# Block 1 of the first segment's input: one load issued by GpSimd instead of two on the sync queue

## The chip, the cores and the metric

The kernel runs on one core of one Trainium2 chip. The metric is the time of one execution on the device, in microseconds (us). A core has TensorE (PE in the profile; PEld is its weight loads), VectorE (DVE), ScalarE (ACT), GpSimd (POOL) and SyncE (SP), which issues transfers. ScalarE and GpSimd can issue transfers as well.

## The reference

Attention with a compressive memory, a gated unit beside it, and a product of the two added to the input. Cut to what matters:

```
xn = layernorm(x)                               # x: 2048 x 640, bf16
q, k, v = xn @ wq, xn @ wk, xn @ wv             # 32 heads of 20
for s in range(4):                              # segments of 512 rows
    p     = softmax(q_s k_s^T * 20**-0.5 + causal mask)
    a_mem = phi(q_s) M / (phi(q_s) z + 1e-6)    # phi(t) = t + 1 if t > 0 else exp(t)
    o_s   = sigmoid(beta) * a_mem + (1 - sigmoid(beta)) * (p v_s)
    M, z  = M + phi(k_s)^T v_s, z + sum(phi(k_s))
s = o @ wo
g = silu((sigmoid(xn @ w_gate) * (xn @ w_up)) @ w_down)   # inner width 1536
out = x + s * g
```

The layer norm at the head is what this change touches: every matmul of a segment needs its normalised and transposed input.

## The kernel before, in words

The rows are worked in four segments of 512, each of four blocks of 128 rows (one row per partition). The order of instructions is written out by hand: each engine executes what is assigned to it in the order in which the code names it, and a wait holds everything behind it on that engine. For the segments after the first a planner with due times mixes attention with the dense matmuls; the first segment has a written-out opening, and that is where the change lies.

`load_x(n, a, b, cols, eng)` (L128 to L132) loads blocks a to b of segment n into the tile `xt`, on the sync queue unless another engine is named; half a block's columns are 80 KB, a whole block 160 KB. `load_wv(half, eng)` (L149 to L151) loads one half of the columns of Wv, 400 KB. `load_w` (L135) loads a whole weight.

The opening issues (L154 to L164), in the order of the code: block 0 in two halves (sync, ScalarE), block 1 in two halves (both sync), the first half of Wv between them (ScalarE), block 2 (sync), block 3 (ScalarE), the second half of Wv, Wk, Wq and beta (sync). GpSimd issues no transfer; it makes constants: `epsc` (L167, the bias of ScalarE's square roots), `mhalf`, `ident` (L173 and L174, the identity for TensorE's transposes), the columns of ones beside V (L184, L185) and `o6` (L506). Then it waits for block 3's normalisation (L191).

TensorE begins with 68 small matmuls on zeros (L640), which do no work of the result. For each block, `half_stats0(j, i)` (L651) takes the statistics of one half's columns on VectorE, `moments0` (L654) joins them, `root0` (L657, ScalarE) and a reciprocal (L662, VectorE) give the inverse deviation, `norm0` (L665) normalises, `transpose0` (L675, TensorE; copies at L678 and L680 on VectorE and ScalarE) transposes, and `do_V` (psv, L121; copy at L352) and then `proj` (psq, L121) multiply. The written order on VectorE runs block 1's first statistics ahead of block 0's normalisation:

```
half_stats0(0, 0); half_stats0(0, 1); moments0(0); root0(0)
half_stats0(1, 0)
norm0(0, (0, CUT), (CUT, D))
half_stats0(1, 1)
moments0(1)
```

The Wg and Wu loads are issued by ScalarE later, between its square roots and copies (L135).

Of the kernel before, what the change touches and what calls it, by code (L numbers as in the profile page):

```python
# [10 lines left out]
D = 640  # L11
# [11 lines left out]
HD = D // 2  # L23
# [52 lines left out]
def kernel(  # L76
# [14 lines left out]
    nc = tc.nc  # L91
# [36 lines left out]
    def load_x(n, a=0, b=4, cols=slice(0, D), eng=nc.sync):  # L128
        if n not in xt_of:
            xt_of[n] = lnp.tile([P, 4, D], BF, name="xt4", bufs=3)  # L130
        src = x2[n * L:(n + 1) * L, :].rearrange("(j p) d -> p j d", p=P)
        eng.dma_start(xt_of[n][:, a:b, cols], src[:, a:b, cols])  # L132
# [16 lines left out]
    def load_wv(half, eng):  # L149
        hs = slice(half * HD, (half + 1) * HD)  # L150
        eng.dma_start(Wv[:, :, hs], A_wv[:, hs].rearrange("(c p) n -> p c n", p=P))  # L151
# [1 line left out]

    load_x(0, 0, 1, slice(0, HD))  # L154
    load_x(0, 0, 1, slice(HD, D), nc.scalar)
    load_x(0, 1, 2, slice(0, HD))
    load_wv(0, nc.scalar)
    load_x(0, 1, 2, slice(HD, D))
    load_x(0, 2, 3)
    load_x(0, 3, 4, eng=nc.scalar)  # L160
    load_wv(1, nc.sync)
# [844 lines left out]
```

## Time and profile before

| what | value |
|---|---|
| median of 3 runs | 317.6 us (317.12 to 317.6) |
| profiled execution | 317.32 us, span 315.6 us |
| TensorE busy | 310.0 us, 98% of the span |
| VectorE, ScalarE busy | 226.0 and 226.8 us, 72% each |
| GpSimd busy | 131.9 us, 42% |
| granted TensorE clock | 1.0 |

Times within the profile count from the start of the span. In the order in time a row gives start, length, engine, line, operation, what it writes and reads, and in brackets the idle time before it with what ended it. The engines' names with a q (SPq, ACTq) are their issues of transfers; the length of such a row is that of the issue, not of the transfer. In the DMA view q1 is the sync queue and q10 ScalarE's, with packets, megabytes and the time that they took as a share of 16 engines.

### The profile page before, as it was taken

The page shows a single profiled execution, that of the slowest core. Times are in us where ns is not written, and L with a number is a line of the kernel's source. Part 1 is how long each engine was busy: PE and PEld are TensorE (multiplying, and loading weights), DVE is VectorE, ACT ScalarE, POOL GpSimd, SP SyncE. Part 2 cuts the span into 40 slices and gives each one's busy share as a digit, 9 for nine tenths or more (in the row PEclk, how much of TensorE's full clock was granted, in tenths as well). Part 3 has the DMA queues.
Part 4 walks back from the last instruction along what each step waited for, and adds up shares of the span by engine and source line. Part 5 has one row for each costly group of instructions (what it writes and reads, how often), then busy time and mean ns, then how long its engine had stood idle before and what let it go on. Part 6 is the DMA issues. An engine that isn't in the chain of part 4 may idle for free.

```text
span 315.6 us, 10262 instructions
## 1 busy us (share of the span) xinstructions
PE 310.0 (98%) x4329; PEld 167.6 (53%) x4329; DVE 226.0 (72%) x512; ACT 226.8 (72%) x231; POOL 131.9 (42%) x227
## 2 busy tenths in 40 slices
PE   7999999999999999999999999999999999999995
PEld 4644445665545445654665454545466655444673
DVE  5573455765868988878879989788777776644575
ACT  3724478778798776778897869679897775777730
POOL 2580035535262534435453364444534353525313
PEclk9999999999999999999999999999999999999999
DMA  7984886410741363504954355139524000280202
GB/s 228 367 351 151 298 214 171 128 42 2 218 154 58 98 150 111 124 23 151 261 168 116 119 98 162 51 111 213 172 84 125 19 23 30 79 159 11 86 21 85
DMA packets 55390, 41.27 MB, mean 131 GB/s; under 512 B 25968, under 2 KB 53968, under 8 KB 55344
## 3 DMA queue, kind: packets, MB, share of 16 engines
q1 hardware_dynamic: 52800, 35.87, 41.0%
q10 hardware_dynamic: 2544, 4.75, 4.1%
q8 instruction: 34, 0.56, 0.7%
q14 instruction: 12, 0.10, 0.1%
HBM read 19.98 MB, written 14.73 MB: 110 GB/s over the span
## 4 chain that ended last, share of the span: by engine, by line
PE 96%; DMA 1%; DVE 1%; SPq 0%; issue 0%
PE up L121 12%; PE yp L121 11%; PE gp L121 11%; PE psq L121 10%; PE Sps L548 8%; PE gp L125 6%; PE yp L125 6%; PE up L125 6%; PE ApsT L572 6%; PE psv L121 5%; PE psq L125 4%; PE sp L121 3%; PE sp L125 3%; PE psv L125 2%; PE sp L532 2%; DMA xt<-in_A_x_dram 1%
## 5 line engine op out<-in xcount | busy, mean ns | idle before, releaser
L556 ACT ACTIVATE pt<-Sps 128x2048 bf16<-128x2048 f32 x80 | 150.3, 1878 | 40.8 <-PE Sps L548 39.5
L558 POOL TENSOR_SCALAR_AFFINE_SELECT pt<-pt 128x512 bf16<-128x512 bf16 x128 | 82.5, 660 | 155.9 <-ACT pt L556 155.8
L435 DVE SCALAR_TENSOR_TENSOR hT<-tg,up 128x512 bf16<-128x512 bf16 x48 | 32.6, 679 | 23.9 <-PE up L121 9.7
L121 PE MATMUL up<-xnT,Wu 128*128 128x512 bf16 x159 | 42.5, 380 | 0.0
L121 PE MATMUL gp<-xnT,Wg 128*128 128x512 bf16 x152 | 40.1, 380 | 0.0
L424 ACT ACTIVATE tg<-gp 128x512 bf16<-128x512 f32 x48 | 28.6, 595 | 14.4 <-PE gp L121 10.5
L121 PE MATMUL yp<-Wd,hT 128*128 128x320 bf16 x246 | 38.2, 300 | 0.0
L548 PE MATMUL Sps<-QT,KT 23*128 23x384 bf16 (+3 forms) x512 | 32.0, 301 | 0.0
L121 PEld LDWEIGHTS <-hT 128*128 128x128 bf16 x246 | 22.7, 98 | 11.3 <-issue 3.0
L580 DVE STREAM_TRANSPOSE tb<-ApsT 128x512 f32<-128x512 f32 x31 | 22.0, 711 | 4.2 <-PE ApsT L572 4.1
L452 DVE SCALAR_TENSOR_TENSOR aa<-t,yp 128x320 bf16<-128x320 bf16 x32 | 15.3, 478 | 13.5 <-ACT t L451 13.4
L125 PE MATMUL gp<-xnT,Wg 128*32 128x512 bf16 x352 | 24.4, 380 | 0.0
L572 PE MATMUL ApsT<-pt,V 128*32 128x512 bf16 (+2 forms) x496 | 23.5, 299 | 0.0
L121 PEld LDWEIGHTS <-Wu 128*128 128x128 bf16 x159 | 14.2, 98 | 17.4 <-issue 4.0
L121 PEld LDWEIGHTS <-Wg 128*128 128x128 bf16 x152 | 14.1, 98 | 15.8 <-issue 1.9
L125 PE MATMUL yp<-Wd,hT 128*32 128x320 bf16 x552 | 21.9, 300 | 0.0
L125 PE MATMUL up<-xnT,Wu 128*32 128x512 bf16 x324 | 21.7, 380 | 0.0
L548 PEld LDWEIGHTS <-KT 23*128 23x128 bf16 x512 | 9.2, 92 | 23.4 <-issue 23.4
L592 DVE STREAM_TRANSPOSE obT<-ob 128x256 f32<-128x256 f32 x31 | 13.5, 434 | 11.1 <-POOL ob L589 11.0
L589 POOL TENSOR_TENSOR ob<-tb,rb 128x320 bf16<-128x320 f32 x27 | 19.9, 737 | 2.3
L121 PE MATMUL psq<-xnT,Wq 128*128 128x512 bf16 x85 | 19.5, 379 | 0.0
L572 PEld LDWEIGHTS <-V 128*32 128x32 bf16 x496 | 14.4, 97 | 8.1 <-ACT tg L424 0.2
(124 smaller groups left out, 448.0 us busy)
## 6 DMA issues: line engine op xcount, KB each, us to landing
KT<-Kd SPq DMA_DIRECT2D x32, 80.0 KB
QT<-Qd SPq DMA_DIRECT2D x32, 80.0 KB
out_dram<-xt SPq DMA_DIRECT2D x14, 160.0 KB
Wg<-in_B_w_gate_dram ACTq DMA_DIRECT2D x1, 1920.0 KB
Wu<-in_B_w_up_dram ACTq DMA_DIRECT2D x1, 1920.0 KB
xt<-in_A_x_dram SPq DMA_DIRECT2D x3, 640.0 KB
Wd<-in_B_w_down_dram SPq DMA_DIRECT2D x1, 1920.0 KB
Od<-odot SPq DMA_DIRECT2D x3, 640.0 KB
```

The source lines that it names most:

```text
L121: nc.tensor.matmul(out_, lhsT=lhsT, rhs=rhs, start=start, stop=stop, skip_group_check=True)
L125: nc.tensor.matmul(out_[cols], lhsT=lhsT[:, cols], rhs=rhs, start=start, stop=stop, tile_position=(0, 32 * r), skip_group_check=True)
L424: nc.scalar.activation(tg[:], gp[:], ACT.Tanh, scale=0.5)
L435: nc.vector.scalar_tensor_tensor(out=h[:], in0=seg[n]["tg"][:], scalar=1.0, in1=up[:], op0=ALU.add, op1=ALU.mult)
L452: nc.vector.scalar_tensor_tensor(out=s["aa"][j][:, hs], in0=t2[:], scalar=1.0, in1=yp[:], op0=ALU.add, op1=ALU.mult)
L548: nc.tensor.matmul(Sps[:, r, c0:c0 + ncol], lhsT=KT[32 * r:32 * r + DH + 3, g, kb * P:(kb + 1) * P], rhs=QT[32 * r:32 * r + DH + 3, g, q0: ...
L556: nc.scalar.activation(pt[:, :, 0:ntot], Sps[:, :, 0:ntot], ACT.Exp, scale=SCALE)
L558: nc.gpsimd.affine_select(out=pt[:, :, c0:c0 + P], in_=pt[:, :, c0:c0 + P], compare_op=ALU.is_ge, fill=0.0, base=0, pattern=[[0, 4], [1, P ...
L572: nc.tensor.matmul(ps[32 * r:32 * r + 32, q0:L], lhsT=Vflat[n % 2][:, off:off + 32], rhs=t[:, r, c0:c0 + ncol], start=(i == 0), stop=(i == ...
L580: nc.vector.transpose(tb[:].rearrange("p h e -> p (h e)"), ps[:].rearrange("p (a t b) -> p a b t", t=32, b=2))
L589: eng.tensor_tensor(to, of, by, op=ALU.mult)
L592: nc.vector.transpose(s["obT", g // 4][:, g % 4, :].bitcast(F32), ob[:].rearrange("p a e b -> p (a e b)").bitcast(F32))
```

## The change

Block 1 of segment 0 is loaded as one transfer of 160 KB that GpSimd issues, at the place of the first of the two halves on the sync queue; the second half's issue goes. As the program is built, that issue is GpSimd's first instruction after the start, ahead of `epsc`; the statistics of block 1's first half wait for this transfer, and those of its second half for nothing more. On the sync queue block 2 comes next after block 0's half. Of the compute instructions none is added, removed or moved on any engine.

```diff
--- before.py
+++ after.py
@@ -153,9 +153,8 @@
 
     load_x(0, 0, 1, slice(0, HD))
     load_x(0, 0, 1, slice(HD, D), nc.scalar)
-    load_x(0, 1, 2, slice(0, HD))
+    load_x(0, 1, 2, eng=nc.gpsimd)
     load_wv(0, nc.scalar)
-    load_x(0, 1, 2, slice(HD, D))
     load_x(0, 2, 3)
     load_x(0, 3, 4, eng=nc.scalar)
     load_wv(1, nc.sync)
```

## The prediction

> **What bounds the kernel now.** I read the page first, for the busy shares and the clock.
>
> ```profile
> span 315.6 us, 10262 instructions
> PE 310.0 (98%) x4329; PEld 167.6 (53%) x4329; DVE 226.0 (72%) x512; ACT 226.8 (72%) x231; POOL 131.9 (42%) x227
> PEclk9999999999999999999999999999999999999999
> ```
>
> TensorE is busy for 310.0 of 315.6 us. Only 5.6 us are not matmul, so an edit of the first loads can matter only by moving the time at which the matmuls get going. The second view is the chain of waits that ended last, in its first 30 us (start, length, what):
>
> ```profile
> 1.71 3.93 DMA xt<-in_A_x_dram
> 5.66 0.50 DVE st L651
> ...
> 7.55 0.45 PE pT L675 x5
> 8.01 1.45 PE psv L121 x10
> 9.46 0.36 PE pT L675 x5
> 9.82 1.36 PE psv L121 x10
> 11.18 0.30 PE pT L675 x5
> 11.47 2.13 PE psv L121 x15
> 13.61 10.79 PE psq L121 x50
> ```
>
> From 7.55 us on the chain is TensorE without a gap (each row starts where the one before ends, up to 24.40). Whatever moves the transposes of block 1 moves the end by the same amount. And the chain begins with one of the two transfers that the edit removes: the second half of block 1, issued at 1.71, landed at 5.64. So the edit sits on the chain, and the question is when block 1 lands.
>
> The third view is the order in time of the first microseconds (start, length, engine, line, operation, and the idle time before it with its cause):
>
> ```profile
> 0.79 0.41 ACTq L132 DMA_DIRECT2D xt<-in_A_x_dram  x1
> 0.79 0.10 POOL L167 MEMSET epsc<- 128x2 f32 x1 [0.29 <-POOLq L990]
> 0.79 1.82 SPq L132 DMA_DIRECT2D xt<-in_A_x_dram  x4
> ...
> 1.14 0.29 POOL L174 TENSOR_SCALAR_AFFINE_SELECT ident<-ident 128x128 bf16<-128x128 bf16 x1
> 1.23 0.46 ACTq L151 DMA_DIRECT2D Wv<-in_A_wv_dram  x1
> ...
> 1.72 0.55 ACTq L132 DMA_DIRECT2D xt<-in_A_x_dram  x1
> ...
> 2.65 0.44 SPq L151 DMA_DIRECT2D Wv<-in_A_wv_dram  x1
> 3.15 0.89 DVE L651 BATCH_NORM_STATS2 st<-xt 128x6 f32<-128x320 bf16 x2 [1.96 <-DMA xt<-in_A_x_dram]
> ...
> 3.59 0.20 ACT L169 ACTIVATE epsc<-epsc 128x1 f32<-128x1 f32 x1
> ...
> 4.19 0.44 DVE L651 BATCH_NORM_STATS2 st<-xt 128x6 f32<-128x320 bf16 x1
> ...
> 4.64 0.16 DVE L662 RECIPROCAL rs<-rs 128x1 f32<-128x1 f32 x1
> 4.84 0.64 DVE L665 TENSOR_SCALAR xn<-xt,mv,rs 128x384 bf16<-128x384 bf16 x2
> ...
> 5.30 0.52 PE L675 MATMUL pT<-ident,xn 128*128 128x128 bf16 x5
> ...
> 5.66 0.49 DVE L651 BATCH_NORM_STATS2 st<-xt 128x6 f32<-128x320 bf16 x1 [0.19 <-DMA xt<-in_A_x_dram]
> ...
> 6.26 0.85 PE L121 MATMUL psv<-Wv,xnT 128*128 128x320 bf16 x5 [0.23 <-ACT xnT L680]
> ...
> 7.55 0.45 PE L675 MATMUL pT<-ident,xn 128*128 128x128 bf16 x5 [0.39 <-DVE xn L665]
> ```
>
> VectorE takes its work in the written order: the two statistics of block 0 (3.15), the first half of block 1 (4.19), then the reciprocal and normalisation of block 0 (4.64 to 5.48), then the second half of block 1 (5.66). The whole wait for block 1 is the 0.19 us before 5.66.
>
> The fourth view is the DMA queues, by packets in a stretch of time. q1 is the sync queue and q10 ScalarE's; the first fence is 2.9 to 4.1 us, the second, the sum over all queues, 4.1 to 5.64 us.
>
> ```profile
> q10 hardware_dynamic: 510, 0.32, 90.5%
> q1 hardware_dynamic: 40, 0.02, 6.6%
> ```
>
> ```profile
> DMA packets 567, 0.48 MB, mean 314 GB/s; under 512 B 54, under 2 KB 567, under 8 KB 567
> ```
>
> For 1.2 us q1 moved almost nothing, 40 packets to q10's 510, though block 1's second half had been issued on it at 1.71. The engines worked off the first half of Wv (issued by ScalarE at 1.23) instead. The sizes, from the list of issues in the page:
>
> ```profile
> Wv<-in_A_wv_dram ACTq DMA_DIRECT2D x1, 400.0 KB
> ...
> xt<-in_A_x_dram SPq DMA_DIRECT2D x3, 80.0 KB
> ...
> xt<-in_A_x_dram SPq DMA_DIRECT2D x1, 160.0 KB
> ```
>
> So what stands on one queue when Wv's turn comes waits for nearly all of Wv. Block 1's first half, issued on SP some 0.46 us earlier (four issues in 1.82 us), got ahead of it; the second half did not.
>
> **The change, part by part.**
>
> *SP.* Two issues go, 2 x 0.455 = 0.91 us of the queue. Block 2 moves up from 2.2 to about 1.24, the second half of Wv from 2.65 to about 1.70, and Wk and Wq follow at about 2.15 and 2.6; as built, neither of these two waits for an earlier load any more. This gains nothing: block 2 is used behind block 1, and the weights stand behind block 2 and Wv in a ring that is full anyway. One thing does change: block 2 (160 KB) now takes the turn ahead of Wv that block 1's first half (80 KB) had.
>
> *GpSimd.* One issue is added, ahead of epsc, mhalf, ident, the ones columns and o6. The trace has no issue by GpSimd. The nearest rows are 0.41 to 0.55 us (ScalarE's) from below; from above I allow 2 us. Its cover: epsc is made at 0.79 and used at 3.59, 2.7 us of slack; ident is ready at 1.43 and used at 5.30. So the engine's own time costs nothing up to 2.7 us, and the excess after that would.
>
> *VectorE's wait.* This is the price. The statistics of the first half now wait for the whole block, and the reciprocal and normalisation of block 0 are queued behind that wait, with TensorE's transposes and ScalarE's copies of block 0 behind them. Let T be the landing of the whole block. If T is 4.19 or less, the second half's statistics follow at 5.47 and no wait is left: 5.47 - 5.66 = -0.19 us, and that is the most the edit can give, since VectorE is then back to back. If T is later, they start at T + 1.28 (5.47 - 4.19), and the shift of the chain is T + 1.28 - 5.66 = T - 4.38. TensorE's own waits (0.23 and 0.39 us) move along with it, since they wait for the same VectorE chain. So nothing takes the shift up again, and it arrives at the end whole. For the longer idle time of TensorE before its first real matmuls I put down no loss of clock: the PEclk row shows 9 in the first slice too, with TensorE idle for its first 1.24 us.
>
> *T itself.* The transfer is issued at 0.79, where epsc stood. SP's first issue, at the same moment, has no packet on record in the first 1.8 us and 17 in the first 1.9 us; in the first 2.5 us q1 has 142, and in the first 2.75 us q10 has 148:
>
> ```profile
> DMA packets 0, 0.00 MB, mean 0 GB/s; under 512 B 0, under 2 KB 0, under 8 KB 0
> ...
> q1 hardware_dynamic: 17, 0.01, 3.2%
> ...
> q1 hardware_dynamic: 142, 0.09, 15.4%
> ...
> q10 hardware_dynamic: 148, 0.09, 10.3%
> ```
>
> So SP's queue needs about 1.05 us from issue to the first data. GpSimd's can't well be quicker: data from 1.8 us at the earliest. The point that decides is when Wv's turn comes on the engines. q10 had its half of block 0 (128 rows) and some small packets done by 2.75, so Wv begins at about 2.7 to 2.9. If block 1's descriptors are there by then, it goes with blocks 0 and 2 and T is about 3.7 to 4.2. If not, it stands where the old second half stood, behind Wv, and T is at least that row's 5.64. It is also later by what stands ahead of it in addition: 80 KB (block 2 for a half block) and 80 KB more of its own, 160 KB at the 314 GB/s of the row, 0.51 us. So T lies between 5.64 and 6.15 and the shift between 1.26 and 1.77 us; I take the middle, 1.5. GpSimd may add up to 0.9 to 1.1 us to SP's 1.05 and still be in time. I take it that it is not: the generation of 128 rows' descriptors by a general engine, and their way to the queues, has to fit into twice the time of the hardware path, cold, as the first thing that GpSimd does.
>
> *A rule that speaks otherwise.* The Trainium skill, in "DMA: Bandwidth & Descriptors", section "Anatomy of one DMA — SWDGE (gpsimd) path", gives a transfer from GpSimd as about 2.0 us fixed plus bytes over 436 GB/s. By that page's figures (an estimate) 160 KB issued at 0.79 land at 0.79 + 2.0 + 0.38 = 3.2, and the sum would be -0.19 us; that fit has no full queue beside it, and no row here shows a GpSimd transfer. Another rule speaks against the edit: the Trainium skill's "SBUF — State Buffer", section "Summary: rules for kernel authors", says to issue such a transfer from ACT or SP, because VectorE's two-port operations starve GpSimd's making of descriptors. Here VectorE is idle for the 1.96 us before 3.15, so by the trace that rule has little to act on in the time that decides.
>
> **The sum.** The profiled execution took 317.32 us, its span 315.6, so 1.7 us lie outside. 317.32 + 0 (SP, GpSimd) + 1.5 = 318.8. The profiled execution is 0.28 below the median of the three runs, 317.6; from that it would be 319.1. I give 318.9.
>
> **The rivals.**
>
> 1. Block 1 behind Wv (my forecast): 317.32 + 1.26 = 318.6 to 317.6 + 1.77 = 319.4. For it: the 1.2 us in which q1 was shut out. Against it: the 0.9 us or more of allowance. Chance 0.54.
>
> 2. Block 1 in time, not slower. The descriptors are ready before 2.7 us, or a third queue gets a share beside Wv instead of waiting for its end. In time gives -0.19: 317.1 to 317.4. A share: from about 3.0 at half of 314 GB/s, 160 KB take 1.0 us, and with the 0.6 us by which block 0's first half landed (3.15) after its 128 packets had gone (2.5) T is 4.6, +0.2: 317.5 to 317.8. In time, Wv's first half moves back by 240 KB, 0.8 us, and takes up the 0.8 us between its landing and its use at 6.26 (a row of the order in time, and one of SP's own waits):
>
> ```profile
> 5.46 0.64 SPq L164 DMA_DIRECT2D beta_b<-in_A_beta_dram  x1
> ...
> SPq L164 <- DMA Wv<-in_A_wv_dram: 1.2, 1, 1.2
> ```
>
> SP's issue of beta had waited for that landing, so it was about 5.45. This rival decides below T = 5.0, where the shift is under 0.2% of the time (0.64 us, about what a measurement of this kernel can tell from no change). Against it: GpSimd's path is the only unknown, and it has to be nearly as quick as SP's. Chance 0.27.
>
> 3. Block 1 behind the second half of Wv as well. SP now issues it at 1.70, and if its queue's turn comes before GpSimd's, block 1 waits for another 400 KB, 1.27 us at 314 GB/s: T of 6.9 to 7.4, shift 2.5 to 3.0, 319.8 to 320.6. A generation that takes 3 us comes out in the same place. Chance 0.14.
>
> 4. Faster by over 0.2%: it would need 0.64 us, and the wait that the edit can remove is 0.19. Only an unseen shift of later transfers would do it. Chance 0.05.
>
> **How the numbers follow.** Slower by over 0.2%: rivals 1 and 3, 0.68. Within: 0.27. Faster: 0.05. The range takes in rival 2 from its best case, 317.1, rival 1 whole, and rival 3 up to 320.4. Rival 1's own range is 318.6 to 319.4.
>
> **What the profile after would show.** Right: the wait before VectorE's statistics of block 1's first half (now at 4.19 without one) ends on the load at 5.6 to 6.2; the second half's statistics show none; the reciprocal of block 0 moves from 4.64 to 6.1 or later; the first gapless row psv moves from 8.01 to about 9.5; from there on the rows are as long as now. A third queue shows its 128 large packets behind most of q10's 640 for Wv. Wrong: the statistics of block 1 back to back from 4.19 with psv at 7.8 (rival 2), or a start of the transfer's packets before 2.7 us. It would be wrong in a way that none of these has if epsc at 3.59 or ident at 5.30 became the late ones, since then GpSimd's own time and not the landing sets the start.

## The result, and the profile after

The changed kernel takes 319.51 us (median of 6 runs, 319.13 to 320.23), the kernel before 317.12 us in the same session (317.04 to 317.6). The ratio is 1.0075, with a 95% interval from 1.0064 to 1.0086: slower by 2.4 us. The profiled execution is one of the slowest of the six, 320.2 us; the text says below what sets it apart.

The page of the changed kernel, the rows that answer to those shown before:

```profile
span 318.5 us, 10263 instructions
PE 311.4 (98%) x4329; PEld 168.4 (53%) x4329; DVE 226.0 (71%) x512; ACT 226.7 (71%) x231; POOL 132.3 (42%) x228
...
PEclk9799999999999999999999999999999999999999
...
q0 software_dynamic: 48, 0.16, 0.1%
```

The span is 2.9 us longer. VectorE and ScalarE are as busy as before, TensorE 1.4 us busier with the same 4329 matmuls, and its clock is down in the second slice (8 to 16 us). A new queue, q0, carries GpSimd's transfer. The order in time (start, length, engine, line, operation; lines below L158 have moved up by one):

```profile
0.80 0.87 SPq L132 DMA_DIRECT2D xt<-in_A_x_dram  x2
...
1.30 0.76 POOL L132 DMA_DIRECT2D xt<-in_A_x_dram  x1 [0.80 <-POOLq L989]
1.72 0.43 SPq L151 DMA_DIRECT2D Wv<-in_A_wv_dram  x1
...
2.07 0.12 POOL L166 MEMSET epsc<- 128x2 f32 x1
...
2.44 0.29 POOL L173 TENSOR_SCALAR_AFFINE_SELECT ident<-ident 128x128 bf16<-128x128 bf16 x1
...
3.60 0.20 ACT L168 ACTIVATE epsc<-epsc 128x1 f32<-128x1 f32 x1
...
6.42 0.49 DVE L650 BATCH_NORM_STATS2 st<-xt 128x6 f32<-128x320 bf16 x1 [2.12 <-DMA xt<-in_A_x_dram]
6.83 0.15 DVE L661 RECIPROCAL rs<-rs 128x1 f32<-128x1 f32 x1
7.01 0.64 DVE L664 TENSOR_SCALAR xn<-xt,mv,rs 128x384 bf16<-128x384 bf16 x2
...
7.03 0.32 PE L634 MATMUL wps<-mn,rs 128*2 128x384 bf16 x1 [1.96 <-DVE rs L661]
...
7.56 0.48 DVE L650 BATCH_NORM_STATS2 st<-xt 128x6 f32<-128x320 bf16 x1
...
9.97 2.60 PE L121 MATMUL psv<-Wv,xnT 128*128 128x320 bf16 x10
```

VectorE waits 2.12 us for the whole block (it had waited 0.19 for the second half), block 0's reciprocal follows at 6.83 instead of 4.64, and the second half's statistics follow with no wait, at 7.56 instead of 5.66: 1.90 us later. TensorE is left idle for 1.96 us, and then the ten psv matmuls take 2.60 us where a group of ten takes 1.5 at full speed. The chain of waits shows both parts:

```profile
1.30 5.09 DMA xt<-in_A_x_dram
...
10.17 2.40 PE psv L121 x10
12.57 0.28 PE pT L674 x5
12.85 1.36 PE psv L121 x10
...
16.64 10.79 PE psq L121 x50
```

psq begins at 16.64 instead of 13.61, 3.03 us later, and from there on its length is the same as before (10.79). Of the 3.03 us, 1.90 are the landing; the rest, 1.13, is the length of the matmuls on the way, the ten psv (2.40 instead of 1.45) above all. That is the clock. The busy times by stretch (us; busy time and count for each engine, then the granted clock) give it for this execution:

```profile
8.00:9.00 1.00, 0.84 (x5) 0.46 (x5) 0.93 (x6) 0.60 (x2) 0.00 (x0) 0.87 1.07 394
9.00:10.00 1.00, 1.00 (x10) 0.70 (x8) 0.96 (x4) 0.43 (x1) 0.00 (x0) 0.50 1.07 370
...
12.00:13.00 1.00, 1.00 (x12) 0.74 (x10) 0.22 (x1) 0.39 (x2) 0.00 (x0) 0.92 0.98 381
```

The clock stands at half from about 8.8 to 12.1 us. Of the six runs three have a mean clock of 1.0 and took 319.13 to 319.36; the three at 0.995 took 319.67 to 320.23. A mean of 1.0 is no proof that the matmuls ran at full speed; the second trace of the changed kernel, below, shows why.

### The profile page after: what moved, and what is told of

Same layout as the page of the kernel before. It is cut to its first block, busy times and chain, and to the rows that moved or that the text cites. A ratio compares the mean times of both kernels' runs of the same rounds, so it can differ in the third digit from the quotient of the medians.

```text
span 318.5 us, 10263 instructions
## 1 busy us (share of the span) xinstructions
PE 311.4 (98%) x4329; PEld 168.4 (53%) x4329; DVE 226.0 (71%) x512; ACT 226.7 (71%) x231; POOL 132.3 (42%) x228
## 4 chain that ended last, share of the span: by engine, by line
PE 96%; DMA 2%; DVE 1%; issue 0%; ACT 0%; POOLq 0%
PE up L121 11%; PE yp L121 11%; PE gp L121 11%; PE psq L121 10%; PE Sps L547 8%; PE gp L125 6%; PE yp L125 6%; PE up L125 6%; PE ApsT L571 5%; PE psv L121 5%; PE psq L125 4%; PE sp L121 3%; PE sp L125 3%; PE psv L125 2%; DMA xt<-in_A_x_dram 2%; PE sp L531 1%
## 5 line engine op out<-in xcount | busy, mean ns | idle before, releaser
L121 PE MATMUL psv<-Wv,xnT 128*128 128x320 bf16 x115 | 19.8, 315 | 0.2 <-ACT xnT L679 0.2
```

The source lines that it names most:

```text
L121: nc.tensor.matmul(out_, lhsT=lhsT, rhs=rhs, start=start, stop=stop, skip_group_check=True)
```

## The experiments

Two theories for the late landing were open. In one GpSimd's transfer stands behind the first half of Wv on the engines that move data ("queue"); in the other GpSimd's own path takes that long ("path"). Beside them: whether it is the whole block or GpSimd that costs, what the order on VectorE adds, and what the clock takes.

**Block 1 whole, on the sync queue.**

```diff
-    load_x(0, 1, 2, eng=nc.gpsimd)
+    load_x(0, 1, 2)
```

> Block 1 whole, as in the change, but issued on the sync queue at the same place; GpSimd issues nothing. If GpSimd's path is the cause, the whole block goes ahead of Wv's turn and has landed by 4.2 us: no wait before the statistics of block 1, 0.2 us faster than before or the same (316.9 to 317.2 us). If the cause is that one whole transfer has to land before VectorE may go on, it lands at 4.6 to 5.2 and the kernel is 0.2 to 0.8 us slower than before.

Measured: 317.07 us against 317.31, ratio 0.9993 (0.9984 to 1.0002). VectorE has no wait before block 1 (the order in time), and the chain has the first psq earlier:

```profile
4.17 0.44 DVE L650 BATCH_NORM_STATS2 st<-xt 128x6 f32<-128x320 bf16 x1
...
5.37 0.49 DVE L650 BATCH_NORM_STATS2 st<-xt 128x6 f32<-128x320 bf16 x1
```

```profile
13.31 6.91 PE psq L121 x32
```

The whole block has landed by 4.17, and psq begins 0.30 us earlier than before. So waiting for a whole block costs nothing; issuing it from GpSimd does. This is the quickest version tried, but its interval takes in 1.

**Only the second half by GpSimd.**

```diff
-    load_x(0, 1, 2, slice(HD, D))
+    load_x(0, 1, 2, slice(HD, D), nc.gpsimd)
```

(against the kernel before)

> As before, with only the second half of block 1 issued by GpSimd and the first half on the sync queue. If the price is that block 0's normalisation is held behind the late landing, it is mostly gone: the second half lands at 6.0 to 6.4 instead of 5.64, and the kernel is 0.4 to 0.8 us slower than before (317.5 to 317.9), at a clock of 1.0. If any transfer by GpSimd here costs the same, it is 2 us or more slower (319.1 or more).

Measured: 317.36 against 317.31, ratio 1.0002 (0.9993 to 1.0011): no change, less than was expected. VectorE's rows:

```profile
5.51 0.49 DVE L651 BATCH_NORM_STATS2 st<-xt 128x6 f32<-128x320 bf16 x1
...
6.45 0.50 DVE L651 BATCH_NORM_STATS2 st<-xt 128x6 f32<-128x320 bf16 x1
```

The half block has landed by 5.51, no later than the sync queue's (5.64). The next wait is a short one, for block 2 at 6.43 by the chain, and normalisation of block 1 begins at 7.04 as before (7.05). So a transfer by GpSimd is not dear as such. It is dear in the change because VectorE's next work needs it at 4.2 us and everything stands behind that wait. (The transfer here is also half as large.)

**No weights beside it.** Both halves of Wv, Wk, Wq and beta go to ScalarE's queue behind block 0's square root; then the same with only the first half of Wv moved, and with only the others moved.

```diff
-    load_wv(0, nc.scalar)
...
-    load_wv(1, nc.sync)
-    load_w(nc.sync, Wk, A_wk)
-    load_w(nc.sync, Wq, A_wq)
-    nc.sync.dma_start(beta_b[:], A_beta.partition_broadcast(P))
...
     root0(0)
+    load_wv(0, nc.scalar)
+    load_wv(1, nc.scalar)
+    load_w(nc.scalar, Wk, A_wk)
+    load_w(nc.scalar, Wq, A_wq)
+    nc.scalar.dma_start(beta_b[:], A_beta.partition_broadcast(P))
```

> The change, with both halves of Wv, Wk, Wq and beta issued by ScalarE only after block 0's square root (about 4.6 us), so that only blocks 0, 2 and 3 are on the queues when GpSimd's transfer comes. Theory queue (it stands behind Wv): its first packet is on record by 2.9 us, as soon as SP's, and it lands by 4.2. Theory path (GpSimd's own path takes that long with nothing in its way): first packet at 4.2 or later as in the change (4.4), landing at 5 or later. The total time says nothing, since the weights come late.

> The change, with only the first half of Wv issued later, by ScalarE after block 0's square root; everything on the sync queue stays. If the first half of Wv alone is what stands ahead, GpSimd's transfer lands at 4.8 as in the run without any weights beside it. If whichever weight is next takes its place, it lands at 5.5 or later. The total time says nothing, since Wv comes late.

> The change, with the second half of Wv, Wk, Wq and beta issued by ScalarE only after block 0's square root; the first half of Wv stays where it is. If the first half of Wv alone holds GpSimd's transfer up, it lands at 5.7 to 6.4 as in the change. If the second half of Wv, now early on the sync queue, has the larger part, it lands by 5.2.

The row of VectorE's wait for block 1, in this order (no weights; first Wv away; the other weights away). Each is one execution; the whole times, 321.56, 325.18 and 319.48 us, are those of kernels whose weights come late and say nothing of the question:

```profile
4.86 0.49 DVE L645 BATCH_NORM_STATS2 st<-xt 128x6 f32<-128x320 bf16 x1 [0.68 <-DMA xt<-in_A_x_dram]
```

```profile
4.89 0.49 DVE L649 BATCH_NORM_STATS2 st<-xt 128x6 f32<-128x320 bf16 x1 [0.74 <-DMA xt<-in_A_x_dram]
```

```profile
5.64 0.49 DVE L646 BATCH_NORM_STATS2 st<-xt 128x6 f32<-128x320 bf16 x1 [1.40 <-DMA xt<-in_A_x_dram]
```

With the first half of Wv away the block lands at 4.87, the same as with no weight at all, although the sync queue's weights stayed. With only the others away it lands at 5.61, near the 5.73 to 6.45 of the kernels with all of them. So the first half of Wv is what stands ahead. But 4.84 is neither theory's number (4.2 or earlier; 5 or later), and without weights q0's first packet is on record between 3.5 and 3.75 us, again between the two (2.9; 4.2): something of the delay was left. One thing that was left is block 3, which moves up into the place of Wv's first half on ScalarE's queue.

**Blocks 0 and 1 alone.** As above, with blocks 2 and 3 moved to ScalarE's later queue too.

> The change, with blocks 2 and 3 and all weights issued by ScalarE only after block 0's square root, so that only block 0's two halves are on the queues beside GpSimd's transfer. Theory path: its first packet is on record at about 3.7 us as in the run without weights, landing 4.6 to 4.8. Theory queue: with nothing in its way it starts by 2.9 and lands by 4.0. The total time says nothing, since the other loads come late.

q0 in the first 2.8 us and in the first 4.0 us, and VectorE's row:

```profile
q0 software_dynamic: 1, 0.01, 0.9%
...
q0 software_dynamic: 48, 0.16, 15.7%
```

```profile
4.12 0.49 DVE L643 BATCH_NORM_STATS2 st<-xt 128x6 f32<-128x320 bf16 x1
```

GpSimd's first packet is on record between 2.75 and 2.8 us, and the block has landed by 4.12 with no wait (0.1 us later than the queue theory's 4.0). So the path alone would be in time; the queue theory holds, with blocks 2 and 3 making the 0.7 us between here and the run without weights. In the changed kernel q0's first packets come between 4.25 and 4.5 us, when q10 has moved most of Wv's first half, about 460 of its 640 packets (the rows are those of the first 4.5 us, with block 0's 144 in q10's count):

```profile
q10 hardware_dynamic: 605, 0.38, 27.3%
q1 hardware_dynamic: 285, 0.24, 26.5%
q0 software_dynamic: 4, 0.02, 1.1%
```

**Block 0's normalisation ahead of block 1's statistics.**

```diff
-    half_stats0(1, 0)
     norm0(0, (0, CUT), (CUT, D))
+    half_stats0(1, 0)
```

(against the changed kernel)

> The change, with the statistics of block 1's first half moved behind block 0's normalisation on VectorE. If the hold-up of block 0 is a part of the price: the two statistics run from 6.4 to 7.4, against 5.66 to 6.15 for the second one before, so about 1.2 us slower than before (318.3), and TensorE has block 0's work between 5.3 and 7.1, so the clock stays at 1.0. If only the landing counts, it is as slow as the change with the clock at 1.0 (319.1 to 319.4).

Measured: 317.97 against 317.31, ratio 1.0019 (1.001 to 1.0028). The hold-up of block 0, with the idle time that it brings TensorE, is the larger part of the price: without it 0.66 us are left. TensorE has block 0's work in the meantime, and its ten psv run at full speed, with the same loads and the same 17 rounds of small matmuls ahead of them. It is less than the 1.2 expected because the block lands at 5.78 here and not at 6.4:

```profile
5.80 0.89 DVE L650 BATCH_NORM_STATS2 st<-xt 128x6 f32<-128x320 bf16 x2 [0.32 <-DMA xt<-in_A_x_dram]
...
8.54 1.37 PE psv L121 x10
```

**TensorE kept busy until block 1 lands.**

```diff
-    keep_warm_columns(17, L // 2)
+    keep_warm_columns(32, L // 2)
```

(against the changed kernel)

> The change with 32 rounds of the four small matmuls on zeros at the start instead of 17, so that TensorE is busy until about 6.7 us instead of 5.06 and the wait for block 1 no longer leaves it idle. Theory clock: the granted clock is 1.0 in every run and the time is that of the change's runs at clock 1.0, 319.1 to 319.4, none near 320.2. If the drop of the clock has nothing to do with the idle time, the spread stays (319.1 to 320.3).

**The changed kernel again**, beside it.

> The changed kernel again, for a second trace beside the others: 319.1 to 320.3 us. The landing of block 1 in this trace (6.39 in the first, 5.78 where only VectorE's order differed) shows how far it moves between executions; the shift of the first gapless psv row should be the landing less 4.38, plus what the clock takes if it drops.

Measured, both against 317.12 us: with 32 rounds 318.55 (318.31 to 319.02, 5 runs), ratio 1.0041 (1.0029 to 1.0053); the changed kernel 319.43 (318.57 to 321.08, 6 runs), ratio 1.0059 (1.0046 to 1.0072). The medians differ by 0.9 us, but the intervals overlap. With 32 rounds all five runs are quicker than the 319.1 to 319.4 expected: that band came from the changed kernel's runs with a recorded clock of 1.0, and the second trace shows that this record doesn't prove full speed. The runs of the changed kernel reach beyond the 319.1 to 320.3 expected at both ends. The traces are plainer: VectorE's wait and the ten psv of the one with 32 rounds; then the first matmuls after the wait in the changed kernel, two rows of its chain, and one stretch of its busy times.

```profile
5.75 0.49 DVE L650 BATCH_NORM_STATS2 st<-xt 128x6 f32<-128x320 bf16 x1 [1.54 <-DMA xt<-in_A_x_dram]
...
9.07 1.52 PE L121 MATMUL psv<-Wv,xnT 128*128 128x320 bf16 x10
```

```profile
6.47 0.49 DVE L650 BATCH_NORM_STATS2 st<-xt 128x6 f32<-128x320 bf16 x1 [2.30 <-DMA xt<-in_A_x_dram]
...
7.08 0.48 PE L634 MATMUL wps<-mn,rs 128*2 128x384 bf16 x1 [2.02 <-DVE rs L661]
...
8.57 1.52 PE L121 MATMUL psv<-Wv,xnT 128*128 128x320 bf16 x5 [0.36 <-ACT xnT L679]
```

```profile
10.73 2.67 PE psv L121 x10
...
17.46 0.22 PE psq L121
```

```profile
9.00:10.00 1.00, 1.00 (x7) 0.57 (x5) 0.93 (x4) 0.00 (x0) 0.00 (x0) 1.00 1.07 366
```

With TensorE busy, ten psv take 1.52 us; in the changed kernel five take 1.52 and the next ten 2.67. And here the granted clock reads 1.00 all along, so the record does not always show matmuls at half speed; their length does. The first matmul after the wait is already slow (0.48 us at 7.08, against 0.32 at 7.03 in the first trace). So here the speed had fallen by then or had never gone up, where in the first trace it fell at 8.8. This execution took 321.08 us, the slowest of its six.

That the speed has to go up first can be read from the small matmuls on zeros at the start, of the kernel before and of the one with 32 rounds:

```profile
1.24 3.82 PE L640 MATMUL wps<-mn 128*32 128x256 bf16 x68 [1.24 <-DVE mn L146]
```

```profile
1.25 5.35 PE L639 MATMUL wps<-mn 128*32 128x256 bf16 x128 [1.25 <-DVE mn L146]
```

The first 68 take 3.82 us, 56 ns apiece; the next 60 add only 1.53 us, 26 ns apiece. Single ones take 419 ns up to 4.5 us and 273 from 5.0 on, and the recorded clock is 1.00 for both. So the changed kernel's small matmuls end, at 5.07, about when TensorE becomes fast.

**A gap in the kernel before, by fewer matmuls on zeros.**

```diff
-    keep_warm_columns(17, L // 2)
+    keep_warm_columns(8, L // 2)
```

(against the kernel before)

> The kernel before, with 8 rounds of the small matmuls on zeros at the start instead of 17: TensorE idles for about 1.8 us (3.05 to 4.86), about as long as the change leaves it idle (1.96), and no load and no wait of VectorE moves. Theory clock: the first real matmuls run at half speed in some executions or all, and the median is 0.5 to 1.8 us above before (317.6 to 318.9). If an idle TensorE costs nothing here, 317.1 to 317.4.

Measured: 319.71 us (318.99 to 320.85) against 317.24, ratio 1.0079 (1.0063 to 1.0095), more than expected. The loads and VectorE stand as before; only the matmuls are longer:

```profile
5.65 0.49 DVE L651 BATCH_NORM_STATS2 st<-xt 128x6 f32<-128x320 bf16 x1 [0.26 <-DMA xt<-in_A_x_dram]
...
6.26 1.52 PE L121 MATMUL psv<-Wv,xnT 128*128 128x320 bf16 x5
```

```profile
1.24 1.90 PE L640 MATMUL wps<-mn 128*32 128x256 bf16 x32 [1.24 <-DVE mn L146]
```

Five psv at 1.52 instead of 0.85: slow first matmuls alone can cost as much as the whole change, with no load moved. It is not the same gap, though. The 32 small matmuls take 59 ns apiece and end at 3.14, before TensorE becomes fast in the run with 32 rounds; so this run does not set apart an idle TensorE and one that was not yet fast. The idle time of the change is better told by the run with block 0 normalised first: the same loads and the same 17 rounds, no long gap, and ten psv in 1.37 us.

**The second half of block 1 ahead of Wv, on ScalarE's queue.**

```diff
+    load_x(0, 1, 2, slice(HD, D), nc.scalar)
     load_wv(0, nc.scalar)
-    load_x(0, 1, 2, slice(HD, D))
```

(against the kernel before)

> As before, with block 1's second half issued by ScalarE ahead of the first half of Wv, in place of the sync queue behind it. Theory turns (what stands behind Wv's turn waits for it): the second half lands by 4.5 us, the wait of 0.19 us goes, 0.2 us faster than before. If Wv, now later, becomes the late one, or the landing does not move: no change.

Measured: 318.32 us (317.64 to 320.54), ratio 1.0052 (1.003 to 1.0073): slower. VectorE's wait is gone (its statistics begin at 5.30), but the loss is where the expectation's other branch had only put "no change":

```profile
8.47 0.96 PE L121 MATMUL psv<-Wv,xnT 128*128 128x320 bf16 x5 [2.57 <-DMA Wv<-in_A_wv_dram]
```

Wv's first half, issued 0.49 us later than before (1.72 instead of 1.23), lands at 8.43 in this execution, where the kernel before had it at about 5.45. Why 0.49 us at the issue become 3 us at the landing isn't settled by one trace, and the trace is of one of the three slowest executions of the ten (320.48 us, all three above 320; the others 317.64 to 319.33). What sets the median isn't seen.

## Why the prediction was right, and where it was not

*The wait (step "VectorE's wait").* Right: the wait is where it was put, before the first half's statistics, and the second half's show none. The formula held to 0.1 us: in the first trace it gives 6.39 - 4.38 = 2.01 and the second statistics moved by 1.90; with 32 rounds it gives 5.73 - 4.38 = 1.35 and they moved by 1.23 (6.89 against 5.66). The formula's 1.28 us is that little too long: from the first half's statistics to the second's it is 1.14 in the first trace (6.42 to 7.56), mostly because the second statistics start 0.55 us after the normalisation, overlapping its end, and not 0.63 (4.84 to 5.47); the reciprocal also follows after 0.41 instead of 0.45 us.

*T itself.* The landing was put at 5.64 to 6.15. Four traces share these loads: the changed kernel's two show 6.39 and 6.45, those with block 0 normalised first and with 32 rounds 5.78 and 5.73. The median of the kernel with 32 rounds, 1.43 us above before, stands for a landing near 5.8 by the formula (1.43 + 4.38). So the mechanism was right, and the size too for a part of the executions. What makes the later pair is open: in them q0's last packets trail until after 6.0 us, in the others q0 is done by 5.5. q0 moved 32 large packets and 16 small ones, not the 128 large ones that were to be seen.

*The size, and luck.* The forecast shift was 1.5 us, 1.77 at most for the first rival; measured are 2.39 (319.51 against 317.12). The measured time lies above this rival's own 318.6 to 319.4, too, and is in the stated range only because that took in the third rival (a shift of 2.5 to 3.0). But the third rival's landing, 6.9 to 7.4, is in no trace, and without the second half of Wv the block still lands at 5.61. The base also helped: 318.9 was counted from 317.32 to 317.6, above the 317.12 that the kernel before took beside the change.

*Why it is late.* The queue was named rightly, the reason for missing its turn was half right. It was argued that descriptors made by GpSimd take too long. Alone, the first packet comes 1.45 to 1.5 us after the issue, against SP's 1.05, which is inside the allowance. But the issue begins at 1.30 and not at 0.79, half a microsecond that the prediction didn't have, and the two together come to 2.8 us, just where Wv's turn begins.

*GpSimd's own time.* Right: 0.76 us for the issue, epsc at 2.07 against its use at 3.60, ident done by 2.73 against 7.45. No one waits for it.

*TensorE's clock.* This is the step that failed: "For the longer idle time of TensorE before its first real matmuls I put down no loss of clock". The PEclk row was read as proof, and it is not one, as a row at 1.00 beside psv of double length shows; the first slice's matmuls themselves ran at about half the rate that the run with 32 rounds reaches later (56 against 26 ns apiece). By the two traces the missing term is 1.1 us (3.03 less 1.90) and 1.8 us (psq at 17.46 in the second trace, 3.85 later than before, of which 2.07 are the landing by the formula). At the median it is about 0.9 (319.43 against 318.55 with TensorE kept busy); this is an estimate, since the intervals overlap and the two traces also land apart (6.45 and 5.73). With it the shift would have been 1.5 + 0.9 = 2.4, against the 2.39 measured. The expected sign that the rows are as long as now from the first psv on failed with it: the ten psv begin at 10.17, not 9.5, and are 0.95 us longer. The Trainium skill, "TensorE: Matmul & The Clock Gate", section "Part 1: The HAM clock gate", says that TensorE's clock is halved by default and after an idle window of some 3.4 us, that the window runs freely, and that the moment of the change therefore differs between runs. The traces agree in that TensorE starts slow and that the moment differs: in the first trace the half-speed stretch begins 3.7 us after TensorE went idle (5.07 to 8.8), in the second the first matmul after the idle time is slow. The idle time here is only 1.96 us, shorter than that window, and no run shows why it is enough. Both traces of the changed kernel have a slow stretch; that some executions escape it can only be guessed from their times (318.57 at the least).

*The rival by the Trainium skill's fit* ("DMA: Bandwidth & Descriptors", section "Anatomy of one DMA — SWDGE (gpsimd) path": 2.0 us and bytes over 436 GB/s, landing at 3.2) did not happen. Even with blocks 0 and 1 alone q0 is not done before 3.75. Half a microsecond of that is the later issue: from 1.30 the fit gives 3.7 (an estimate by that page), against a landing by 4.12 alone and at 5.73 to 6.45 beside all the other loads.

## What to carry to other kernels

Ask of a moved transfer not how long its path is but which large transfer's turn it misses: GpSimd's transfer landed by 4.12 us by itself and 1.6 to 2.3 us later beside the first half of Wv and the rest, and Wv itself landed 3 us later in one trace after an issue 0.49 us later. Then ask what is queued behind the wait on the engine that needs it; the second half of a block by GpSimd was free where the whole one held up everything. And price the idle time of TensorE at the start of a kernel by the length of its matmuls, since the recorded clock can read 1.00 while they run at half speed. The small matmuls ahead of them have to bridge the wait: 32 rounds did, 17 did not.

## What the runs showed of the hardware

- GpSimd's first transfer began 0.5 us after the first ones of SP and ScalarE (1.30 against 0.79), kept GpSimd for 0.76 us and, with only block 0 beside it, had its first packet 1.45 to 1.5 us after its begin.
- It moved its 160 KB in 32 large packets and 16 small ones, 48 in all, where q1 had 288 for half a block and a block (two transfers of 128 rows).
- The granted clock was 1.00 in the records of an execution whose psv matmuls took 0.27 us each instead of 0.14, and for the first small matmuls of the run with 32 rounds (419 ns each) as for its later ones (273 ns).
